# Value products of a head in two query tiles instead of three, and its output product in the same head

## The chip, the cores and the metric

The kernel runs on one core of a Trainium2 chip. The metric is the device time of one execution in microseconds, and lower is better. The core's engines work in parallel, each through its own queue in program order: TensorE (PE, with weight loads shown as PEld), VectorE (DVE), ScalarE (ACT), GpSimd (POOL) and SyncE (SP, which issues most DMAs).

## The reference

Three layers follow each other: a masked attention, a mixture of eight experts with one expert a token, and a gated feed-forward layer. The change touches the first, whose core is

```
q, k, v: (2, 8, 768, 64)                 # batches, heads, tokens, width of a head
mask   = bucket(q) == bucket(k)          # 6 hash bits of a token: (q @ proj > 0)
scores = where(mask, q @ k.T / 8, -1e9)
attn   = exp(scores - max); attn = attn / (sum + 1e-9)
out    = attn @ v                        # becomes x (1536, 512) of the experts
logits = x @ w_gate; gates of the output: x @ w_output_gate
```

The router's choice of an expert (the largest logit) needs all eight heads of a batch.

## The kernel before

**Tiling of the attention.** The 16 heads (two batches of eight) run one after the other, each in six query tiles of 128 tokens, `t` = 0 to 5. A step `g = 6 h + t` of the main loop issues the work below in the order in which it is written; every engine runs its share in that order.

1. `scores(g + 1)`: four matmuls into one of two PSUM buffers (`ps_s`) for the next tile; hash bits ride in the product, so that tokens of other buckets come out far away. `smax(g + 1)` on DVE: a minimum over 768 columns (L166) and a small scaling (L167), both needed by the exponential.
2. In tile 1, `hash_mm` of the next head. In tiles 1, 3 and 5, value products of the head before (`av_step`, L203): two of its six key tiles each (`AV_AT`), which add up in one PSUM buffer, the only one of the pool `ps_a`. Each writes 64 columns of the array, two halves side by side.
3. In tile 4, `o_out(h - 2)`: the output product (L255), which undoes the transposition and adds the router's logits, into the only buffer of the pool `ps_m`, and its two products with 1/sum on DVE (L264, L265).
4. `tposes(g, half)`: six transposes (L188) of the tile's exponentials into two PSUM buffers, and their eviction on ACT (L192) or DVE (L194), as the table `K["ev"]` says for each of the twelve halves of a head (1 is DVE).
5. `side(pos)`: the exponential of the next tile on ACT (`sexp`, L175) ahead of the transposes' evictions (position 0, tiles 1, 3 and 5) or behind them (position 2, tiles 0, 2 and 4); the splits of a later head's q and k into a rounded part on ACT (`split_a`, L105) and a rest on DVE and POOL (`split_b`, L117 to L121).
6. In tile 5, behind the transposes, `o_evac(h - 1)`: the value products leave PSUM (L234), and the sums of the exponentials are inverted (L238, L239).

Transposes of a tile wait for its exponential, the exponential for the scaling, that for the minimum, that for the scores. The last head, 15, differs: value products of head 14 lie in its tiles 0, 1 and 2, output products in tiles 0 and 3, and its own value products follow in tiles 4 and 5.

Between these lie the small operations of the router of the first batch (`todo`, one entry a tile from head 10, tile 2), and from head 14 on copies, splits and weight splits on POOL and ACT for the second stage (`extra`). Where POOL shall not begin before DVE's scaling is done, a copy of one column into `held` stands ahead of it.

Of the kernel before, what the change touches and what calls it, by code (L numbers as in the profile page):

```python
# [7 lines left out]
F32 = mybir.dt.float32  # L8
# [7 lines left out]
ALU = mybir.AluOpType  # L16
# [5 lines left out]
S, D, NB, NH = 768, 64, 2, 8  # L22
NT = 6
N, DM, E, FF, F2 = 1536, 512, 8, 1024, 1536
C = 224
GR = ((0, 6), (6, 4), (10, 2))
K = {'se': (2, 0, 2, 0, 2, 0), 'se0': (0, 1, 2, 1, 1, 2), 'ev': (0, 0, 0, 1, 0, 1, 0, 0, 0, 0, 1, 0), 'ev0': (0, 0, 0, 1, 0, 1, 0, 0, 0, 1, 0, 0), 'ev1': (0, 0, 0, 1, 0, 1, 0, 0, 0, 1, 0, 1), 'avl': (5,), 'oul': 0, 'hml': 0, 'hc': ((0, 0), (0, 2), (1, 1), (2, 1)), 'sa': ((0, 2), (2, 2)), 'sb': ((1, 0), (2, 2)), 'sa0': ((2, 2), (4, 1)), 'sb0': ((3, 2), (5, 0)), 'hm0': 0, 'hc0': ((1, 0), (1, 2), (3, 0), (4, 1))}
C_ID, C_TRI, C_THR, C_REV, C_TOK, C_IOTA, C_BASE, C_SLOT = 0, 128, 256, 258, 266, 278, 279, 287
CW = C_SLOT + C
FAR = 1024.0  # L30
AV_AT = {1: (0, 1), 3: (2, 3), 5: (4, 5)}


@with_exitstack
def attn_moe_kernel(ctx: ExitStack, tc: tile.TileContext, xin, cst, projd, wblk, wmoe, w2in, out):
# [127 lines left out]
    def smax(g):  # L163
        m = mm[:, g % 4]
        sb = sm.tile([128, 2], F32, tag="sb", name="sb")
        DVE.tensor_reduce(out=m[:, 1:2], in_=st[g][:, :, :384], axis=AX.XY, op=ALU.min)  # L166
        DVE.scalar_tensor_tensor(  # L167
            out=sb, in0=m[:, 1:2].to_broadcast([128, 2]), scalar=BIG / 2, in1=m, op0=ALU.is_le, op1=ALU.mult
        )
        scl[g], nbs[g] = sb[:, 0:1], sb[:, 1:2]  # L170
        last[0] = sb[:, 0:1]
# [24 lines left out]
    av = {}  # L196
# [21 lines left out]
    def halves(ap):  # L218

        return ap.bitcast(U16).rearrange("p t (n a) -> p t a n", a=2)  # L220

    def to_planes(t0, nt, hh, src):
        o = x_q.bitcast(U16).rearrange("p t (a n) -> p t a n", a=2)[:, t0:t0 + nt, :, hh * 64:(hh + 1) * 64]
        POOL.tensor_copy(o, src)

    def late_planes(hh, t0=0, nt=6):
        to_planes(t0, nt, hh, halves(x_b)[:, t0:t0 + nt, :, hh * 64:(hh + 1) * 64])
# [3 lines left out]
    def o_evac(h, q=None, copy=DVE.tensor_copy):  # L231
        n = q[1] * 128 if q else 384
        o = sm.tile([128, n], F32, tag="o" if q is None else f"o{n}", name="o", bufs=2 if q is None else 1)
        copy(o, av.pop((h, q) if q else h)[:, :n])  # L234
        oT[h, q] = o
        t0, nt = q or (0, NT)
        r = sm.tile([128, NT], F32, tag="r", name="r", bufs=2)
        DVE.tensor_reduce(out=r[:, :nt], in_=sums[:, h * 6 + t0:h * 6 + t0 + nt], axis=AX.X, op=ALU.add)  # L238
        DVE.reciprocal(r[:, :nt], r[:, :nt])  # L239
        rs[h, q] = r  # L240

    def o_out(h, q=None):
        b, hh = divmod(h, NH)
        o, r = oT.pop((h, q)), rs.pop((h, q))
        p = ps_m.tile([128, 512], F32, tag="m", name="m")
        t0, nt = q or (0, NT)
        t = slice(b * 6 + t0, b * 6 + t0 + nt)
        lp = sm.tile([128, nt, 16], F32, tag=f"lp{nt}", name="lp", bufs=2) if hh else lg[:, t]
        if b:
            xo = x_b[:, t0:t0 + nt, hh * 64:(hh + 1) * 64]  # L250
        else:
            xf = xo = sm.tile([128, 6, 64], F32, tag="xf", name="xf", bufs=2)
        if q is None:
            for j in range(3):
                PE.matmul(p[:, j * 160:(j + 1) * 160], o[:, j * 128:(j + 1) * 128], wb[:, hh], start=True, stop=True)  # L255
            ps = p[:, :480].rearrange("p (j c n) -> p j c n", j=3, c=2)
            rr = r.rearrange("p (c j) -> p j c", c=2).unsqueeze(3)
            lo, xo, sh = lp.rearrange("p (c j) n -> p j c n", c=2), xo.rearrange("p (c j) n -> p j c n", c=2), [128, 3, 2]
        else:
            for j in range(nt):  # L260
                PE.matmul(p[:, j * 80:(j + 1) * 80], o[:, j * 128:(j + 1) * 128], wl, start=True, stop=True)
            ps = p[:, :nt * 80].rearrange("p (j n) -> p j n", j=nt)
            rr, lo, sh = r[:, :nt].unsqueeze(2), lp, [128, nt]
        DVE.tensor_tensor(out=lo, in0=ps[..., 64:], in1=rr.to_broadcast(sh + [16]), op=ALU.mult)  # L264
        DVE.tensor_tensor(out=xo, in0=ps[..., :64], in1=rr.to_broadcast(sh + [64]), op=ALU.mult)  # L265
        if hh:
            (DVE if hh >= NH - 2 else POOL).tensor_tensor(out=lg[:, t], in0=lg[:, t], in1=lp, op=ALU.add)
        if not b:
            to_planes(0, 6, hh, halves(xf))
        elif NH + 3 <= h < L:  # L270
            late_planes(hh)

    def router(gi):
        t0, n = GR[gi]
# [362 lines left out]
    with tc.manual_schedule():  # L637
# [72 lines left out]
        L = NHD - 1  # L710
# [4 lines left out]
                f()  # L715
            return g

        parts = []

        def split_behind(d):  # L720
            def g():
# [18 lines left out]
        for g in range(NG):  # L740
            h, t = divmod(g, NT)
            if t == 1 and h + 3 < NHD:
                load(h + 3)
            if g + 1 < NG:
                scores(g + 1)
                smax(g + 1)
            if g < NT:
                set_up(g)
            if 2 * NT <= g < 2 * NT + (E * C + N) // 256:
                for i in (g - 2 * NT,):  # L750
                    nc.sync.dma_start(
                        out=xr[i * 256:(i + 1) * 256].rearrange("(p r) d -> p r d", p=128),
                        in_=zeros[0].bitcast(U32).unsqueeze(1).to_broadcast([128, 2, 512]),
                    )
            if g == 6 * NT:
                for n in range(4):
                    for part in range(2):
                        w_load(n, part)
            if g == 10 * NT + 1:
                r = router(0)  # L760
                todo = [r["s1"], r["s1b"], None, lambda: (r["s2"](), r["s2c"]()), r["s2b"], r["s4"], r["s4b"]]
                for f in r["sc"]:
                    todo += [f, None]
                todo += [r["s4c"], None, None, None, r["s3a"], None, r["s3b"], None, None, None, r["s5"]]
            early, late = [], []
            if h < L:
                if t == (1 if h else 0):
                    early.append(lambda: hash_mm(h + 1))
                if h:
                    for k in AV_AT.get(t, ()):  # L770
                        early.append(lambda k=k: av_step(h - 1, k))
                if h > 1 and t == 4:
                    (late if K["oul"] else early).append(lambda: o_out(h - 2))
            elif t < 3:
                av_step(h - 1, 2 * t)
                av_step(h - 1, 2 * t + 1)
                if t == 0:
                    o_out(h - 2)
                if t == 2:
                    o_evac(h - 1)  # L780
            elif t == 3:
                o_out(h - 1)
            else:
                k = 3 * (t - 4)
                av_group(h, qa, (k, k + 1, k + 2))
                if t == 5:
                    o_evac(h, qa)
            for f in early:
                f()
            if h and h < L and t == 5 and not K["avl"].count(5):  # L790
                o_evac(h - 1)
            if g > 10 * NT + 1 and todo:
                f = todo.pop(0)
                if f:
                    f()

            def side(pos):
                if g + 1 < NG and K["se" if 0 < h < L else "se0"][t] == pos:
                    sexp(g + 1)
                if h < L and (t, pos) == (1, 0):  # L800
                    hash_codes(h + 1)
                for i in range(2):
                    if h + 2 < NHD and K["sa" if h > 1 else "sa0"][i] == (t, pos):
                        split_a(h + 2, i)
                    if h + 2 < NHD and K["sb" if h > 1 else "sb0"][i] == (t, pos):
                        if t == 5:
                            POOL.tensor_copy(held, last[0])
                        split_b(h + 2, i)

            side(0)  # L810
            tposes(g, 0)
            side(1)
            tposes(g, 1)
            for f in late:
                f()
            if h and h < L and t == 5 and K["avl"].count(5):
                o_evac(h - 1)
            side(2)
            for f in extra.get((h - L + 1, t), ()):
                f()  # L820
        o_out(L, qa)
        av_group(L, qb, tuple(range(NT)))
        ra, rb = router(1), router(2)
        ra["s1"]()
# [11 lines left out]
        ra["s2c"]()  # L836
        for t in (6, 7, 8):
            x0_hot(DVE, t)
        o_out(L, qb)
        for t in (6, 7, 8):  # L840
            x0_add(t)
        rb["s1"]()
# [659 lines left out]
```

## Time and profile before

| | |
|---|---|
| median of 3 runs | 722.79 us (722.61 to 722.83) |
| profiled execution | 724.47 us |
| its span, first to last instruction | 722.7 us |
| mean granted clock of TensorE | 0.994 |
| PE, DVE, ACT, POOL busy | 705.2, 556.8, 448.1, 283.4 us |

All but the first line come from one profiled execution, which is 1.7 us longer than the median. Busy times are shares of the whole span, of which the attention stage is the first third; the ends of matmuls are modelled, so that the starts of instructions say more of PE than its busy time.

### The profile page before, as it was taken

Reading aid. Unit: us, or ns where it says so; the run is one execution under the profiler, and the core shown is the slowest. Engines: PE = TensorE matmul, PEld = TensorE weight load, DVE = VectorE, ACT = ScalarE, POOL = GpSimd, SP = SyncE. Lnnn points to the kernel's source line nnn. Section 1 sums busy time; section 2 is a strip of 40 time slices with the busy share of each in tenths; the row PEclk is TensorE's granted clock in tenths of the full one; section 3 lists DMA queues with packets and bytes.
Section 4 is the critical chain, followed back from the end, with each engine's and each line's share of the span. In section 5 each row is a group of like instructions: output and inputs, shape, how many; then the busy total and the mean of one; then the engine's idle time right before and its main releaser. Section 6 shows DMA issues by size and latency. Waiting matters only on the chain.

```text
span 722.7 us, 13158 instructions
## 1 busy us (share of the span) xinstructions
PE 705.2 (98%) x4505; PEld 604.2 (84%) x4506; DVE 556.8 (77%) x1105; ACT 448.1 (62%) x962; POOL 283.4 (39%) x316
## 2 busy tenths in 40 slices
PE   7899999999999999999999999999999999999995
PEld 6667667667766699999999999999999999999994
DVE  5777887789777778788888878886886877777644
ACT  5787877787877637677778766575444453444320
POOL 4243334322556348845443303333322332223224
PEclk9999999999999999999999999999999999999998
DMA  7348261123212038699899741132121222122013
GB/s 241 107 164 308 85 222 59 59 65 112 104 49 64 15 128 254 174 257 213 237 288 245 229 129 59 40 107 88 59 62 55 88 76 71 55 63 59 0 51 127
DMA packets 53432, 88.01 MB, mean 122 GB/s; under 512 B 19872, under 2 KB 23280, under 8 KB 53360
## 3 DMA queue, kind: packets, MB, share of 16 engines
q1 hardware_dynamic: 50688, 80.61, 37.7%
q0 software_dynamic: 2304, 6.31, 2.3%
q8 instruction: 37, 0.61, 0.3%
q14 instruction: 35, 0.29, 0.1%
q10 hardware_dynamic: 368, 0.20, 0.1%
HBM read 69.65 MB, written 13.12 MB: 115 GB/s over the span
## 4 chain that ended last, share of the span: by engine, by line
PE 84%; issue 4%; DVE 4%; POOL 2%; DMA 2%; ACT 2%; SPq 0%; POOLq 0%; ACTq 0%; DVEq 0%
PE tp L188 9%; PE av L203 8%; PE y L1033 6%; PE s L161 4%; PE s L160 4%; PE h L995 4%; PE h L994 4%; PE h L993 3%; PE aba L1270 3%; PE aba L1272 3%; PE abb L1270 3%; PE aba L1271 3%; PE abb L1272 3%; PE abb L1271 3%; PE y L1034 3%
## 5 line engine op out<-in xcount | busy, mean ns | idle before, releaser
L166 DVE TENSOR_REDUCE mm<-s 128x1 f32<-128x768 f32 x96 | 91.1, 949 | 26.7 <-PE s L161 25.8
L175 ACT ACTIVATE p<-s,sb 128x768 f32<-128x768 f32 x96 | 95.0, 989 | 21.2 <-DVE sb L167 20.4
L188 PEld LDWEIGHTS tp<-cs,p 128*128 128x128 f32 x576 | 64.9, 141 | 37.9 <-ACT p L175 24.4
L188 PE MATMUL tp<-cs,p 128*128 128x128 f32 x576 | 82.7, 280 | 6.4 <-DMA cs<-cst 2.9
L516 DVE TENSOR_TENSOR wl<-wr,wh 128x512 fp32r<-128x512 f32 x125 | 83.2, 705 | 4.9 <-ACT wh L515 1.1
L192 ACT ACTIVATE pt<-tp 128x384 f32<-128x384 f32 x143 | 65.1, 487 | 34.7 <-PE tp L188 34.7
L964 POOL TENSOR_TENSOR pc<-t,pc 128x256 fp32r<-128x256 f32 x38 | 33.1, 873 | 134.8 <-ACT pc L963 119.2
L1033 PE MATMUL y<-hl,wh 128*128 128x448 f32 x224 | 75.0, 378 | 0.6 <-DVE hl L1007 0.5
L515 ACT ACTIVATE wh<-wr 128x512 fp32r<-128x512 f32 x128 | 73.7, 624 | 1.3 <-DMA wr<-wmoe 1.2
L160 PE MATMUL s<-tk,tq 76*128 76x384 f32 x192 | 73.7, 384 | 0.3 <-DVE tq L137 0.3
L994 PE MATMUL h<-xl,wh 128*128 128x224 f32 x256 | 70.3, 275 | 0.5 <-DVE xl L450 0.3
L995 PE MATMUL h<-xh,wl 128*128 128x224 f32 x256 | 70.6, 276 | 0.0
L993 PE MATMUL h<-xh,wh 128*128 128x224 f32 x256 | 70.3, 275 | 0.2 <-ACT xh L449 0.2
L203 PE MATMUL av<-pt,v 128*64 128x384 f32 x360 | 68.0, 499 | 0.2 <-DVE r L238 0.2
L161 PE MATMUL s<-bk,bq 128*128 128x384 f32 x192 | 65.6, 342 | 0.0
L1034 PE MATMUL y<-hl,wl 128*128 128x224 f32 x224 | 59.5, 266 | 0.0
L964 POOL TENSOR_TENSOR pc<-s,pc 128x256 fp32r<-128x256 f32 x44 | 38.0, 875 | 33.0 <-ACT pc L963 32.0
L118 POOL CAST bq<-tq 64x768 fp32r<-64x768 f32 x15 | 21.2, 1414 | 74.8 <-ACT tq L105 47.4
L1160 ACT ACTIVATE gh<-p 128x384 fp32r<-128x384 f32 x21 | 11.0, 526 | 63.2 <-DVE p L1289 63.2
L993 PEld LDWEIGHTS h<-xh,wh 128*128 128x128 f32 x256 | 48.9, 191 | 1.5 <-ACT xh L449 0.4
L994 PEld LDWEIGHTS h<-xl,wh 128*128 128x128 f32 x256 | 49.1, 192 | 1.0 <-DVE xl L450 0.5
L203 PEld LDWEIGHTS av<-pt,v 128*64 128x64 f32 x360 | 21.9, 136 | 32.8 <-issue 24.5
(264 smaller groups left out, 2002.6 us busy)
## 6 DMA issues: line engine op xcount, KB each, us to landing
wr<-wmoe SPq DMA_DIRECT2D x128, 256.0 KB
r<-w2in SPq DMA_DIRECT2D x36, 512.0 KB
x<-xin SPq DMA_DIRECT2D x30, 384.0 KB
xr<-zero SPq DMA_DIRECT2D x13, 512.0 KB
v<-xin SPq DMA_DIRECT2D x16, 192.0 KB
wb<-wblk SPq DMA_DIRECT2D x1, 640.0 KB
x<-xin SPq DMA_DIRECT2D x3, 192.0 KB
tq<-code SPq DMA_DIRECT2D x30, 18.0 KB
```

The costliest lines, as they stand in the source:

```text
L160: PE.matmul(p[:, c, :384], T[h, 0][:76, qs], T[h, 1][:76, sl], start=True, stop=False)
L161: PE.matmul(p[:, c, :384], B[h, 0][:, qs], B[h, 1][:, sl], start=False, stop=True)
L166: DVE.tensor_reduce(out=m[:, 1:2], in_=st[g][:, :, :384], axis=AX.XY, op=ALU.min)
L175: ACT.activation(p.rearrange("p (c n) -> p c n", c=2), st.pop(g)[:, :, :384], ACTF.Exp, scale=scl.pop(g), bias=nbs.pop(g), accum_out=sums[ ...
L188: PE.transpose(ps[:, j * 128:(j + 1) * 128], pt_[g][:, k * 128:(k + 1) * 128], ident)
L203: PE.matmul(av[h][c * 64:(c + 1) * 64, :384], v, PT[h][:, k, c * 384:(c + 1) * 384], start=(k == 0), stop=(k == NT - 1), skip_group_check= ...
L516: eng.tensor_tensor(out=l, in0=r, in1=h.bitcast(F32), op=ALU.subtract)
L993: PE.matmul(ps, wh, xh, start=first, stop=False)
L994: PE.matmul(ps, wh, xl, start=False, stop=False)
L995: PE.matmul(ps, wl, xh, start=False, stop=last)
L1033: PE.matmul(p, wh[:, w], hl, start=(f == 0), stop=False, skip_group_check=True)
L1034: PE.matmul(p[:, 0], wl[:, w], hl[:, 0], start=False, stop=(f == 7), skip_group_check=True)
```

## The change

- Value products of the head before go into tiles 1 and 3 alone, three key tiles each.
- `o_evac` follows directly behind the second group, in tile 3; within it the sums come ahead of the copy.
- The output product goes to tile 5 of the same head (`o_out(h - 1)` instead of `o_out(h - 2)`), ahead of the transposes, and for heads 0 to 13 into the buffer of `ps_a` that held the value products. Its products on DVE are returned as a function `take` and issued in tile 0 of the next head, behind the minimum and scaling there.
- In tile 5 both evictions are on DVE (before one on DVE, one on ACT).
- The split of k's rest goes from position 2 of tile 2 to position 0 of tile 3, with the `held` copy ahead of it; the latter is now also placed in tile 3 of heads 0 and 1.
- The router's operations begin two tiles earlier.

```
-K = {... 'ev': (0, 0, 0, 1, 0, 1, 0, 0, 0, 0, 1, 0), ... 'sb': ((1, 0), (2, 2)), ...}
+K = {... 'ev': (0, 0, 0, 1, 0, 1, 0, 0, 0, 0, 1, 1), ... 'sb': ((1, 0), (3, 0)), ...}
-AV_AT = {1: (0, 1), 3: (2, 3), 5: (4, 5)}
+AV_AT = {1: (0, 1, 2), 3: (3, 4, 5)}
...
     def o_evac(h, q=None, copy=DVE.tensor_copy):
-        copy(o, av.pop((h, q) if q else h)[:, :n])
...
         rs[h, q] = r
+        copy(o, av.pop((h, q) if q else h)[:, :n])
...
     def o_out(h, q=None):
-        p = ps_m.tile([128, 512], F32, tag="m", name="m")
+        if h < L - 1:
+            p = ps_a.tile([128, 512], F32, tag="a", name="m")
+        else:
+            p = ps_m.tile([128, 512], F32, tag="m", name="m")
...
-        DVE.tensor_tensor(out=lo, in0=ps[..., 64:], in1=rr.to_broadcast(sh + [16]), op=ALU.mult)
-        DVE.tensor_tensor(out=xo, in0=ps[..., :64], in1=rr.to_broadcast(sh + [64]), op=ALU.mult)
...
+        def take():
+            DVE.tensor_tensor(out=lo, in0=ps[..., 64:], in1=rr.to_broadcast(sh + [16]), op=ALU.mult)
+            DVE.tensor_tensor(out=xo, in0=ps[..., :64], in1=rr.to_broadcast(sh + [64]), op=ALU.mult)
...
+        return take
...
                 scores(g + 1)
                 smax(g + 1)
+            if t == 0 and takes:
+                takes.pop()()
...
-            if g == 10 * NT + 1:
+            if g == 9 * NT + 5:
...
-                if h > 1 and t == 4:
-                    (late if K["oul"] else early).append(lambda: o_out(h - 2))
+                if h and t == 3:
+                    early.append(lambda: o_evac(h - 1))
+                if h and t == 5:
+                    early.append(lambda: takes.append(o_out(h - 1)))
             elif t < 3:
                 av_step(h - 1, 2 * t)
                 av_step(h - 1, 2 * t + 1)
-                if t == 0:
-                    o_out(h - 2)
...
-            if h and h < L and t == 5 and K["avl"].count(5):
-                o_evac(h - 1)
```

## Rows read from the trace of the kernel before

**Rows 1.** Windows of head 6, tiles 1, 2, 4, 5: stretch, length, then each engine.

```profile
101.41:105.14 3.73, 3.73 (x28) 1.91 (x28) 3.34 (x7) 3.46 (x8) 1.14 (x1) 1.00 0.33 101
105.14:106.50 1.36, 1.36 (x11) 1.33 (x11) 1.21 (x2) 0.58 (x2) 0.42 (x1) 1.00 1.01 384
...
109.45:111.64 2.19, 2.19 (x18) 2.19 (x18) 1.60 (x3) 1.53 (x6) 2.02 (x2) 1.00 0.00 0
111.64:114.60 2.96, 2.96 (x20) 1.75 (x20) 2.15 (x6) 2.42 (x6) 1.21 (x2) 1.00 0.02 6
```

**Rows 2.** Timeline of PE in tiles 4 and 5: start, duration, instructions merged.

```profile
109.63 0.34 PE L161 MATMUL s<-bk,bq 128*128 128x384 f32 x1
109.81 0.98 PE L255 MATMUL m<-wb,o 128*128 128x160 f32 x6
110.62 0.82 PE L188 MATMUL tp<-cs,p 128*128 128x128 f32 x6
...
111.81 0.34 PE L161 MATMUL s<-bk,bq 128*128 128x384 f32 x1
```

**Rows 3.** Timeline of all engines: a softmax from its last score matmul, then value products.

```profile
105.31 0.34 PE L161 MATMUL s<-bk,bq 128*128 128x384 f32 x1
...
105.69 0.96 DVE L166 TENSOR_REDUCE mm<-s 128x1 f32<-128x768 f32 x1 [0.15 <-PE s L161]
...
106.68 0.16 DVE L167 SCALAR_TENSOR_TENSOR sb<-mm 128x2 f32<-128x2 f32 x1
106.76 0.55 DVE L194 COPY pt<-tp 128x384 f32<-128x384 f32 x1
106.94 0.99 ACT L175 ACTIVATE p<-s,sb 128x768 f32<-128x768 f32 x1 [0.43 <-DVE sb L167]
...
107.32 0.14 PEld L203 LDWEIGHTS av<-pt,v 128*64 128x64 f32 x2 [0.18 <-issue]
107.64 0.14 PEld L203 LDWEIGHTS av<-pt,v 128*64 128x64 f32 x2 [0.18 <-issue]
```

**Rows 4.** Timeline in head 14, where transposes waited for the exponential.

```profile
224.69 0.99 ACT L175 ACTIVATE p<-s,sb 128x768 f32<-128x768 f32 x1 [1.06 <-DVE sb L167]
...
225.83 0.44 PE L188 MATMUL tp<-cs,p 128*128 128x128 f32 x2 [0.25 <-ACT p L175]
```

**Rows 5.** Timeline of head 6: POOL's cast, the scaling, the output's second product.

```profile
110.71 0.82 POOL L121 CAST bk<-tk 64x768 fp32r<-64x768 f32 x1
111.00 0.55 DVE L167 SCALAR_TENSOR_TENSOR sb<-mm 128x2 f32<-128x2 f32 x1
...
111.64 0.54 DVE L265 TENSOR_TENSOR xf<-m,r 128x384 f32<-128x384 f32 x1
```

**Rows 6.** Windows of heads 1, 10 and 11, 12, and 14 with tile 0 of 15.

```profile
28.33:43.18 14.85, 14.08 (x93) 9.31 (x93) 10.49 (x19) 11.60 (x25) 4.03 (x5) 1.00 0.32 109
...
159.62:189.39 29.77, 29.66 (x207) 20.69 (x206) 25.93 (x59) 23.07 (x48) 11.19 (x10) 1.00 0.26 90
...
189.39:203.96 14.57, 14.57 (x100) 10.26 (x99) 11.43 (x23) 11.39 (x25) 7.57 (x7) 1.00 0.36 128
218.52:236.08 17.56, 17.14 (x114) 11.61 (x113) 12.86 (x28) 13.63 (x31) 12.37 (x19) 1.00 0.21 65
```

**Rows 7.** Timeline of heads 14 and 15: cast, two subtractions on POOL, router.

```profile
230.31 0.63 ACT L515 ACTIVATE wh<-wr 128x512 fp32r<-128x512 f32 x1
...
231.03 1.28 POOL L516 TENSOR_TENSOR wl<-wr,wh 128x512 fp32r<-128x512 f32 x1 [0.26 <-ACT wh L515]
...
232.40 1.81 POOL L398 TENSOR_TENSOR xh<-x_b,xh 128x768 fp32r<-128x768 f32 x1
...
238.26 0.19 DVE L372 TENSOR_REDUCE rt_s<-rt_ed 128x6 f32<-128x48 f32 x1
```

**Rows 8.** Windows of head 0: stretch, length, busy times; third from last: granted clock.

```profile
11.21:14.63 3.42, 0.60 (x6) 0.63 (x7) 1.68 (x3) 2.08 (x5) 2.21 (x2) 1.00 1.01 389
14.63:18.04 3.41, 3.41 (x16) 3.31 (x15) 1.71 (x4) 1.92 (x4) 1.77 (x4) 0.50 0.83 260
```

More of the change, by code (lines that the diff above doesn't have):

```diff
@@ L26 @@
 GR = ((0, 6), (6, 4), (10, 2))
-K = {'se': (2, 0, 2, 0, 2, 0), 'se0': (0, 1, 2, 1, 1, 2), 'ev': (0, 0, 0, 1, 0, 1, 0, 0, 0, 0, 1, 0), 'ev0': (0, 0, 0, 1, 0, 1, 0, 0, 0, 1, 0, 0), 'ev1': (0, 0, 0, 1, 0, 1, 0, 0, 0, 1, 0, 1), 'avl': (5,), 'oul': 0, 'hml': 0, 'hc': ((0, 0), (0, 2), (1, 1), (2, 1)), 'sa': ((0, 2), (2, 2)), 'sb': ((1, 0), (2, 2)), 'sa0': ((2, 2), (4, 1)), 'sb0': ((3, 2), (5, 0)), 'hm0': 0, 'hc0': ((1, 0), (1, 2), (3, 0), (4, 1))}
+K = {'se': (2, 0, 2, 0, 2, 0), 'se0': (0, 1, 2, 1, 1, 2), 'ev': (0, 0, 0, 1, 0, 1, 0, 0, 0, 0, 1, 1), 'ev0': (0, 0, 0, 1, 0, 1, 0, 0, 0, 1, 0, 0), 'ev1': (0, 0, 0, 1, 0, 1, 0, 0, 0, 1, 0, 1), 'hml': 0, 'hc': ((0, 0), (0, 2), (1, 1), (2, 1)), 'sa': ((0, 2), (2, 2)), 'sb': ((1, 0), (3, 0)), 'sa0': ((2, 2), (4, 1)), 'sb0': ((3, 2), (5, 0)), 'hm0': 0, 'hc0': ((1, 0), (1, 2), (3, 0), (4, 1))}
 C_ID, C_TRI, C_THR, C_REV, C_TOK, C_IOTA, C_BASE, C_SLOT = 0, 128, 256, 258, 266, 278, 279, 287
@@ L263, in o_out @@
             rr, lo, sh = r[:, :nt].unsqueeze(2), lp, [128, nt]
-        DVE.tensor_tensor(out=lo, in0=ps[..., 64:], in1=rr.to_broadcast(sh + [16]), op=ALU.mult)
-        DVE.tensor_tensor(out=xo, in0=ps[..., :64], in1=rr.to_broadcast(sh + [64]), op=ALU.mult)
[L266 to L271, printed above, removed]
+        def take():
+            DVE.tensor_tensor(out=lo, in0=ps[..., 64:], in1=rr.to_broadcast(sh + [16]), op=ALU.mult)
+            DVE.tensor_tensor(out=xo, in0=ps[..., :64], in1=rr.to_broadcast(sh + [64]), op=ALU.mult)
+            if hh:
+                (DVE if hh >= NH - 2 else POOL).tensor_tensor(out=lg[:, t], in0=lg[:, t], in1=lp, op=ALU.add)
+            if not b:
+                to_planes(0, 6, hh, halves(xf))
+            elif NH + 3 <= h < L:
+                late_planes(hh)
+        return take
     def router(gi):
@@ L716, in behind @@
             return g
-        parts = []
+        parts, takes = [], []
         def split_behind(d):
@@ L764, in attn_moe_kernel @@
                 todo += [r["s4c"], None, None, None, r["s3a"], None, r["s3b"], None, None, None, r["s5"]]
-            early, late = [], []
+            early = []
             if h < L:
@@ L781, in attn_moe_kernel @@
             elif t == 3:
-                o_out(h - 1)
+                o_out(h - 1)()
             else:
@@ L789, in attn_moe_kernel @@
                 f()
-            if h and h < L and t == 5 and not K["avl"].count(5):
-                o_evac(h - 1)
-            if g > 10 * NT + 1 and todo:
+            if g > 9 * NT + 5 and todo:
                 f = todo.pop(0)
@@ L805, in side @@
                     if h + 2 < NHD and K["sb" if h > 1 else "sb0"][i] == (t, pos):
-                        if t == 5:
+                        if t in (3, 5):
                             POOL.tensor_copy(held, last[0])
@@ L813, in attn_moe_kernel @@
             tposes(g, 1)
-            for f in late:
-                f()
-            if h and h < L and t == 5 and K["avl"].count(5):
-                o_evac(h - 1)
             side(2)
@@ L820, in attn_moe_kernel @@
                 f()
-        o_out(L, qa)
+        o_out(L, qa)()
         av_group(L, qb, tuple(range(NT)))
@@ L838, in attn_moe_kernel @@
             x0_hot(DVE, t)
-        o_out(L, qb)
+        o_out(L, qb)()
         for t in (6, 7, 8):
```

## The prediction

> **What bounds the kernel now.** I read the page first: TensorE (PE) is shown busy for 705.2 of 722.7 us, but ends of matmuls are modelled there, so this alone doesn't say that nothing is lost. The change touches only the attention stage, which runs from about 9 to 250 us. I therefore cut one settled head into its query tiles, with the windows laid from one score matmul to the next tile's [rows 1]. The reader should see that each tile's length is a plain sum: a tile with scores and transposes alone takes 1.36 us; one with an output product as well 2.19; one with value products of two key tiles 2.96; the one with the hash product and value products 3.73. The two tiles not shown take 1.36 and 2.95, and the head 14.57 us. Then I followed PE in order of time through the same head [rows 2]: group follows group with no hole. So in a settled head PE sets the pace, and the other engines have slack: DVE 11.4 and ACT 11.4 of 14.57 us [rows 6]. Such a head gets faster only if PE gets less to do, and slower as soon as a result comes late for PE.
>
> **What the change takes away.** Value products write 64-column blocks of the array, the groups around them full width. Two key tiles are four pairs of matmuls, a pair every 0.32 us (weight loads at 107.32 and 107.64 [rows 3]), 1.28 in all, yet the tile grows by 2.96 - 1.36 = 1.60 us [rows 1]. So 0.32 us is paid for going in and out of such a group. Before there are three groups a head, after two with three key tiles each. The bounds are 0.28 and 0.34; I take 0.32, in 14 heads (1 to 14): -4.5 us.
>
> **What it moves together.** The work of PE is now uneven: tiles 1 and 3 (the second and fourth) carry all value products, tile 5 only the output product (2.19 - 1.36 = 0.83 us), tiles 4 and 0 nothing. Between the last score matmul of tile 5's scores and its first transpose lie: transposes of tile 4, the next scores, the output product. From rows: score to the next full-width group 0.18 (109.63 to 109.81), transposes and scores 111.81 - 110.62 = 1.19, last score through the output product to the transposes 110.62 - 109.63 = 0.99; together 2.36 us [rows 2]. Before, a value group lay in it as well.
>
> What must happen in that time is the softmax: the minimum on DVE starts 0.38 us after the last score matmul, takes 0.96, the small scaling ends at 106.84, the exponential starts at 106.94 and takes 0.99 [rows 3]: 1.63 to its start, 2.62 to its end. Where PE waited for nothing else, transposes start 0.15 us after the exponential's end [rows 4]. That makes 2.77 us with no queue at all. So PE waits 2.77 - 2.36 = 0.41 us ahead of the transposes of tile 5, in every one of the 14 heads: +5.7 us. The bounds are 0.35 (a few hundredths less at each hand-over) and 0.8: the scaling ends late when GpSimd (POOL) is in the middle of an instruction, as at 111.00, where it took 0.55 instead of 0.16 and ended as POOL's cast did [rows 5]. There the cast ended (111.53) 1.90 us after the scores of tile 5; with two more pairs of value products ahead of these scores (0.64) that becomes 1.26, and the scaling starts at 0.38 + 0.96 + 0.03 = 1.37, so they miss each other by 0.1 us. The next tile's softmax has the same 2.77 us and comes out just in time, behind the same wait.
>
> The rest of the edits costs nothing in a settled head. The seventh DVE eviction of a head (0.55 [rows 3]) and its partner fall into that wait, and end as the next minimum can start. The products on DVE, put off to tile 0, follow that minimum and scaling and end 1.53 [rows 3] + 0.63 [rows 5] = 2.16 us after their scores; the value products, which need their PSUM buffer, come at 1.36 + 0.18 + the hash product's 3.73 - 2.96 = 2.31 at the earliest. That cover is 0.15 us; without it each tenth goes to PE. The evacuation in tile 3 is on DVE behind nothing but the end of the value products, and the next minimum is queued behind it 0.9 us later. POOL's split in tile 3 starts when ACT has delivered, as before. So a settled head goes from 14.57 to 14.57 - 0.32 + 0.41 = 14.66 us.
>
> **Where heads are not settled.** Heads 2 to 9, 12 and 13: 10 x 0.09 = +0.9 us. Heads 10 and 11 hold the router's small operations, and take 29.77 us together [rows 6], 0.63 more than two settled ones. Moved forward two tiles, its matmuls on PE stay (0.2, an estimate: a third of the 0.63), and its DVE work falls where there is room: 2 x 14.66 + 0.2 = 29.52, -0.2. Head 1 had no output product and waits (14.85 [rows 6]); now it has one, and ACT's split of 768 columns lies between two evictions in tile 4, ahead of the exponential. I estimate it at 0.7 us, since a cast of 512 takes 0.63 [rows 7]. The wait there is then about 1.0 instead of 0.41: 15.25, +0.4.
>
> Head 14 with tile 0 of head 15 is dearer. There the value products are still in tile 0, directly behind the scores, and now they need the buffer that the put-off products are to free. Counted from the scores of tile 5: the second minimum of head 15 starts after four small router operations (about 0.85 us in a chain, the first with 0.19 is shown [rows 7]) and two evictions, at 4.8, and ends at 5.7. Its scaling meets POOL: the exponential ends at 2.6, ACT's cast (0.63) follows, POOL's subtraction (1.28) and its next one (1.81) [rows 7] run until 6.6. The products take 0.63 more after the scaling (111.55 to 112.18 [rows 5]): the buffer is free at 7.3, while PE could start at 4.2. PE waits 3.1 us; without meeting POOL it is 2.4. The page SBUF — State Buffer of the Trainium skill, section Who interferes with whom, says that a DVE operation with two SBUF inputs and a POOL operation that reads SBUF exclude each other for a whole instruction; [rows 5] agree for a cast, and for the longer subtraction the rule gives the 3.1. A scaling that didn't wait would give the 2.4, and a sum smaller by 0.7 us. The stretch took 17.56 [rows 6], with 0.6 of waits of its own in it that go; after: 14.66 + 1.60 for the group in tile 0 + 3.13 = 19.39, +1.8.
>
> **The sum.** +0.9 - 0.2 + 0.4 + 1.8 = +2.9 us. After the attention stage a chain follows that starts from its last tiles, so nothing catches this up. The profiled execution took 724.47 us with a span of 722.7; its successor should take 727.4. The runs had a median of 722.79, and the same difference gives 725.7.
>
> **Rivals.**
> The waits ahead of tile 5 are hidden (ends on the other side). Then 14 x 0.41 = 5.7 us fall away: 720.0. It decides from 0.21 us a head down, where the total is nil. For it: before, no settled head waits. Against it: the 2.77 us are counted on rows without a queue, and PE can't fill 2.36 us with more than it has.
>
> The wait in head 15 is small, because the put-off products reach DVE earlier than I have them. With 3.1 us gone the total is -0.2, 722.6; with half gone 724.1, both about unchanged. For it: it rests on the order in four queues that I put together by hand. Against it: even an idle POOL leaves 2.4 us.
>
> The clock falls in that wait. TensorE was granted 1.00 up to 14.63 us and 0.50 (1.2 of 2.4 GHz) from there to 18.04, after a stretch in which it was busy for 0.60 of 3.42 us [rows 8]. Three idle microseconds in head 15 resemble that. PE's work of 3.41 us at half the clock costs 1.7 more: 727.4. The page TensorE: Matmul & The Clock Gate of the Trainium skill, Part 1, has the clock throttled by default and released by activity, which the two rows agree with; by that rule this change is dangerous in that place only. Against it: scores stand close ahead of the wait and value products behind it.
>
> POOL's cast does meet the scaling in tile 5, by a tenth of slip. It costs up to 0.39 more in some 12 heads: +4.7, 730.4. Only the margin of 0.1 us speaks against it.
>
> **How the numbers follow.** Within 0.2% (1.4 us) is about what a measurement can't tell from no change. The forecast (724.3 to 727) has 0.47, the fallen clock 0.15, the meeting with POOL 0.06: slower 0.68. The small wait in head 15 has 0.15, and I add 0.05 for errors that cancel: same 0.20. The hidden waits have 0.12. The range leaves out those and the meeting with POOL: from 722.4, below the small wait, to 728.3, above the fallen clock with the forecast's own error. The likeliest case's own range is 724.3 to 727.
>
> **What would show it.** Tiles of a settled head should last 1.36, 4.38, 1.36, 3.59, 1.36 and 2.59 us. Transposes of tile 5 should start 0.15 us after the exponential's end, with PE idle some 0.4 us ahead. In head 15 the first value products should start right behind the put-off products on DVE, some 3 us late. The prediction is wrong if tile 5 takes 2.2 us, if the value products in head 15 aren't held, or if the heads 2 to 9 lose much more than a tenth each.

## The result, and the profile after

The changed kernel takes 733.36 us (median of 4 runs, 730.8 to 734.59) against 722.81 us for the kernel before: the ratio is 1.0142, with a 95% interval of 1.0114 to 1.0169. It is slower, as forecast, but by 10.5 us instead of 2.9, and outside the range. The profiled execution took 733.75 us with a span of 731.9.

I cut the same head as in [rows 1] into windows, one from the last score matmul of a tile to that of the next (tiles 1, 2, 3, 4, 5 and 0).

```profile
102.18:106.56 4.38, 4.38 (x32) 2.20 (x31) 3.95 (x8) 3.59 (x7) 2.03 (x3) 1.00 0.44 158
106.56:107.93 1.37, 1.37 (x12) 1.33 (x11) 1.18 (x3) 0.49 (x1) 0.00 (x0) 1.00 0.68 247
107.93:111.53 3.60, 3.60 (x24) 2.04 (x24) 2.47 (x7) 3.35 (x7) 1.58 (x2) 1.00 0.05 9
111.53:112.89 1.36, 1.36 (x12) 1.33 (x11) 0.96 (x1) 0.86 (x3) 1.26 (x2) 1.00 0.04 12
112.89:115.53 2.64, 2.39 (x18) 2.15 (x17) 1.94 (x5) 2.22 (x5) 0.00 (x0) 1.00 0.00 0
115.53:116.99 1.46, 1.46 (x12) 1.27 (x11) 1.35 (x3) 0.82 (x4) 0.00 (x0) 1.00 0.00 0
```

Four tiles are what was forecast (4.38, 1.36, 3.59, 1.36), and tile 5 is the only one in which PE isn't busy throughout. The head takes 14.81 us instead of 14.55. Tile 5 in the timeline, PE with what it waits for (start, duration, instructions merged):

```profile
112.89 0.34 PE L161 MATMUL s<-bk,bq 128*128 128x384 f32 x1
...
112.89 0.16 DVE L167 SCALAR_TENSOR_TENSOR sb<-mm 128x2 f32<-128x2 f32 x1
113.06 0.98 PE L258 MATMUL m<-wb,o 128*128 128x160 f32 x6
113.15 0.99 ACT L175 ACTIVATE p<-s,sb 128x768 f32<-128x768 f32 x1
...
114.29 0.88 PE L188 MATMUL tp<-cs,p 128*128 128x128 f32 x6 [0.25 <-ACT p L175]
114.32 0.16 DVE L167 SCALAR_TENSOR_TENSOR sb<-mm 128x2 f32<-128x2 f32 x1
114.60 0.99 ACT L175 ACTIVATE p<-s,sb 128x768 f32<-128x768 f32 x1 [0.37 <-DVE sb L167]
```

From the output product to the transposes it is 1.23 us, where it was 0.81 [rows 2]: the wait is 0.42, and the transposes start 0.15 us after the exponential's end at 114.14. They take 0.88 us instead of 0.82. The exponential of tile 0 starts 0.12 us after its scaling and ends at 115.59; the transposes of tile 0 start 0.14 us behind it, at 115.73, and tile 0 is 0.09 longer as well.

The dearest place is tile 0 of head 15:

```profile
235.97 0.33 PE L161 MATMUL s<-bk,bq 128*128 128x384 f32 x1
...
236.65 1.80 POOL L405 TENSOR_TENSOR xh<-x_b,xh 128x768 fp32r<-128x768 f32 x1
...
237.49 0.98 DVE L167 SCALAR_TENSOR_TENSOR sb<-mm 128x2 f32<-128x2 f32 x1
...
238.56 0.54 DVE L270 TENSOR_TENSOR x_b<-m,r 128x384 f32<-128x384 f32 x1
...
239.24 2.19 PE L203 MATMUL av<-pt,v 128*64 128x384 f32 x6 [2.94 <-DVE x_b L270]
...
239.91 0.27 PEld L203 LDWEIGHTS av<-pt,v 128*64 128x64 f32 x2 [0.37 <-issue]
...
240.55 0.27 PEld L203 LDWEIGHTS av<-pt,v 128*64 128x64 f32 x2 [0.37 <-issue]
```

The value products wait for the put-off products, and those for a scaling that lasts 0.98 us and ends when POOL's subtraction does (238.45). The pairs then follow each other 0.64 us apart, twice the 0.32 of [rows 3]. Windows over that place show what else changed there (the third value from the end is the granted clock):

```profile
234.49:237.90 3.41, 1.57 (x10) 1.26 (x10) 3.04 (x10) 2.42 (x6) 2.62 (x3) 1.00 0.06 10
237.90:241.31 3.41, 2.07 (x8) 0.85 (x8) 1.20 (x3) 1.08 (x2) 3.09 (x6) 0.50 0.18 67
241.31:244.73 3.42, 3.42 (x14) 2.31 (x10) 0.00 (x0) 0.98 (x2) 0.16 (x1) 0.50 0.00 0
```

PE's clock was granted at 0.50, 1.2 of 2.4 GHz, for 6.8 us, after a stretch in which it was busy for 1.57 of 3.41 us. Head 1 and heads 10 and 11 together, to be held against the first two of [rows 6], 14.85 and 29.77 us:

```profile
27.25:42.73 15.48, 14.71 (x99) 10.30 (x99) 11.06 (x20) 11.11 (x23) 4.34 (x6) 1.00 0.31 104
161.60:192.51 30.91, 29.85 (x206) 20.77 (x206) 26.42 (x63) 22.74 (x45) 10.82 (x13) 1.00 0.26 87
```

With the start of the last score matmul of each head's tile 2 as the border, the attention stage grows by 0.63 us in head 1, 2.43 in heads 2 to 9, 1.14 in heads 10 and 11, 0.69 in heads 12 and 13, and 4.42 in head 14 with tile 0 of head 15: 9.3 us. Behind that lie 1.2 us more, half of them behind the last matmul. The two spans differ by only 9.2, because the profiled execution of before took 1.25 us more up to that border in head 1; its clock was low there [rows 8], and that of after was not.

### The profile page after: what moved, and what is told of

Read it like the earlier page. It is cut to its first block, busy times and chain, and to the rows that moved or that the text cites. A ratio compares the mean times of both kernels' runs of the same rounds, so it can differ in the third digit from the quotient of the medians.

```text
span 731.9 us, 13181 instructions
## 1 busy us (share of the span) xinstructions
PE 707.0 (97%) x4505; PEld 606.0 (83%) x4506; DVE 561.1 (77%) x1119; ACT 446.4 (61%) x948; POOL 278.1 (38%) x330
## 4 chain that ended last, share of the span: by engine, by line
PE 78%; POOL 5%; DVE 5%; issue 5%; ACT 4%; DMA 1%; SPq 0%; POOLq 0%; ACTq 0%; DVEq 0%
PE av L203 8%; PE tp L188 8%; PE y L1036 5%; PE s L160 4%; PE s L161 3%; PE aba L1273 3%; PE h L998 3%; PE aba L1275 3%; PE abb L1273 3%; PE aba L1274 3%; PE abb L1275 3%; PE abb L1274 3%; PE h L996 3%; PE h L997 3%; PE q L1203 3%
## 5 line engine op out<-in xcount | busy, mean ns | idle before, releaser
L175 ACT ACTIVATE p<-s,sb 128x768 f32<-128x768 f32 x96 | 95.0, 990 | 19.9 <-DVE sb L167 15.6
L192 ACT ACTIVATE pt<-tp 128x384 f32<-128x384 f32 x129 | 58.5, 488 | 45.9 <-PE tp L188 45.6
L203 PE MATMUL av<-pt,v 128*64 128x384 f32 x360 | 66.2, 503 | 3.1 <-DVE x_b L270 2.9
L203 PEld LDWEIGHTS av<-pt,v 128*64 128x64 f32 x360 | 23.5, 138 | 37.8 <-issue 30.1
L998 PEld LDWEIGHTS h<-xh,wl 128*128 128x128 f32 x256 | 49.2, 192 | 0.0
```

The source lines that it names most:

```text
L175: ACT.activation(p.rearrange("p (c n) -> p c n", c=2), st.pop(g)[:, :, :384], ACTF.Exp, scale=scl.pop(g), bias=nbs.pop(g), accum_out=sums[ ...
L203: PE.matmul(av[h][c * 64:(c + 1) * 64, :384], v, PT[h][:, k, c * 384:(c + 1) * 384], start=(k == 0), stop=(k == NT - 1), skip_group_check= ...
L998: PE.matmul(ps, wl, xh, start=False, stop=last)
```

## The experiments

The kernel before ran beside each of them. Its median was 723.96 us beside the first three runs told here and the one with work put into the wait; 723.46 beside the runs on the second eviction of tile 4, the value products alone, the router's old place and the earlier scores; 723.16 beside the two with spread steps and the eviction given back; and 723.17 beside the two with steps in DVE's gaps. Ratios are to that kernel.

**The wait in head 15 taken away.** The output product of head 13 uses the pool `ps_m`, as before the change, so that the value products of head 14 wait for nobody.

```
-        if h < L - 1:
+        if h < L - 2:
             p = ps_a.tile([128, 512], F32, tag="a", name="m")
```

> The changed kernel with the output product of head 13 in its own PSUM buffer, so that the value products in tile 0 of head 15 need not wait for the put-off products. If that wait of 3 us and the half clock behind it are a part of the loss, 4 to 6 us come back: 727.5 to 729.5 us, no stretch of half clock near 238 us, tile 0 of head 15 at about 3 us instead of 8.3. If the loss there has another cause (a late exponential, POOL's work), PE waits for that instead and at most 1 us comes back.

727.85 us, ratio 1.0062 (1.0045 to 1.0078). Tile 0 of head 15, 8.33 us long in the changed kernel, falls to its plain work, and the clock stays:

```profile
235.95:238.91 2.96, 2.96 (x20) 1.75 (x19) 2.83 (x6) 1.27 (x3) 2.69 (x4) 1.00 0.24 89
```

So this one place costs 5.4 us, half of the whole loss. To part wait and clock, the next run keeps the wait and fills it.

**The wait kept, the clock held.** 48 matmuls into an unread buffer stand ahead of the value products in tile 0 of head 15.

```
+                if t == 0:
+                    busy = ps_m.tile([128, 512], F32, tag="m", name="busy")
+                    for _ in range(48):
+                        PE.matmul(busy[:, :128], ones, ones, start=True, stop=True)
                 av_step(h - 1, 2 * t)
```

> The changed kernel with 48 small matmuls, whose result nobody reads, ahead of the value products in tile 0 of head 15: some 2.7 us of work in the place of the wait. If the wait is for the put-off products, the value products start no later. If the fall of the clock costs something of its own, it no longer falls, and 2 to 3 us come back: 730 to 731.5 us. If the clock costs nothing beyond the wait, the time stays at 733.

731.6 us, ratio 1.011 (1.0092 to 1.0128), a tenth above the 730 to 731.5 us expected. The window of the tile in this kernel:

```profile
235.11:241.07 5.96, 5.73 (x67) 4.52 (x67) 2.99 (x6) 2.67 (x6) 5.18 (x8) 1.00 0.13 47
```

The value products still wait 0.23 us for the put-off products behind the 48 matmuls, so the added work is no longer than the wait. 5.96 - 2.96 = 3.0 us is the wait, as forecast (3.13), and 8.33 - 5.96 = 2.4 us went with the clock that fell. Here it stays at 1.00.

The 2.4 us are one execution's. The run further down with work put into the wait has the same code in head 15 and the same wait of 3.0 us, and its tile 0 took 7.55 us, 1.6 more than with the clock held:

```profile
236.70:244.25 7.55, 4.62 (x19) 2.84 (x19) 2.99 (x6) 2.99 (x6) 5.17 (x8) 0.77 0.13 35
```

Its clock was at 0.50 for 3.4 us instead of 6.8. In the two runs with a shorter minimum the tile took 7.47 and 7.40 us. So the clock cost 1.4 to 2.4 us in four executions with the same wait.

**The softmax of tiles 5 and 0 made shorter.** The minimum is taken over half of the columns there, in heads 1 to 15.

```
+        c = 1 if g % NT in (0, 5) and g > NT else 2
-        DVE.tensor_reduce(out=m[:, 1:2], in_=st[g][:, :, :384], axis=AX.XY, op=ALU.min)
+        DVE.tensor_reduce(out=m[:, 1:2], in_=st[g][:, 2 - c:, :384], axis=AX.XY, op=ALU.min)
```

> The changed kernel with the minimum of the scores taken over 384 of the 768 columns in tiles 5 and 0 of heads 1 to 15: this leaves out half of the maximum, and shortens the softmax there by 0.4 us. If the waits ahead of the transposes of tiles 5 and 0 (0.41 us, and 0.14 by two smaller ones) make a settled head 14.81 instead of 14.24, most of it goes: tile 5 at 2.2 to 2.3 us, tile 0 at 1.36 to 1.4, a head at 14.25 to 14.4, the run at 726 to 728. If PE or another engine sets the pace, a head stays at 14.8 and the run at 733.

729.47 us, ratio 1.0087 (1.0064 to 1.011): a settled head takes 14.56 us, so only half of what was expected came. The minimum is 0.40 shorter, but the scaling of tile 5 takes 0.37 us instead of 0.16 and ends with POOL's cast (111.86 and 111.85), and the exponential starts 0.12 us behind it, after two evictions on ACT. The next run takes one of these evictions away.

**The second eviction of tile 4 on DVE, on top of that.**

```
-'ev': (0, 0, 0, 1, 0, 1, 0, 0, 0, 0, 1, 1)
+'ev': (0, 0, 0, 1, 0, 1, 0, 0, 0, 1, 1, 1)
```

> The changed kernel with the shorter minimum of the run before (384 columns in tiles 5 and 0, half of the maximum left out), and besides with the second eviction of tile 4 on DVE instead of ACT. If two chains of almost equal length reach the exponential of tile 5, one over the minimum and one over the two evictions that stand ahead of it on ACT, then both are now shorter: tile 5 falls from 2.49 to 2.2 us and a settled head to 14.24 to 14.3. If the rest of the wait has another cause, tile 5 stays at 2.5.

727.75 us in the one run, and 14.52 us a head instead of 14.24 to 14.3: a second miss. Its timeline shows what still holds the exponential:

```profile
109.90 0.82 POOL L121 CAST bk<-tk 64x768 fp32r<-64x768 f32 x1
...
110.38 0.36 DVE L168 SCALAR_TENSOR_TENSOR sb<-mm 128x2 f32<-128x2 f32 x1
...
110.83 0.99 ACT L176 ACTIVATE p<-s,sb 128x768 f32<-128x768 f32 x1 [0.23 <-DVE sb L168]
110.95 0.98 PE L259 MATMUL m<-wb,o 128*128 128x160 f32 x6
...
111.97 0.44 PE L189 MATMUL tp<-cs,p 128*128 128x128 f32 x2
```

With an earlier minimum the scaling meets POOL's cast, the rival that I had at 0.06, and ends with it (110.74 and 110.72). The wait is still 1.02 - 0.81 = 0.21 us; in the changed kernel the cast ends 0.04 us before the scaling starts.

**Work put into the wait.** Seven matmuls into an unread buffer in tile 5 of heads 2 to 13.

```
+            if t == 5 and 1 < h < L - 1:
+                busy = ps_m.tile([128, 512], F32, tag="m", name="busy")
+                for _ in range(7):
+                    PE.matmul(busy[:, :128], ones, ones, start=True, stop=True)
```

> The changed kernel with 7 small matmuls (about 0.39 us of PE's time, result unread) behind the output product in tile 5 of heads 2 to 13. If PE waits there anyway for the exponential, a head stays at 14.8 and the run within 1 us of the changed kernel. If PE's own work sets the pace, each of the 12 heads grows by 0.4 and the run by 4.7 us.

732.84 us, ratio 1.0119 (1.0096 to 1.0141), with settled heads of 14.81 us to the hundredth. PE had nothing to do there.

**The value products moved alone.** The kernel before with two groups of three key tiles and nothing else of the change.

```
-AV_AT = {1: (0, 1), 3: (2, 3), 5: (4, 5)}
+AV_AT = {1: (0, 1, 2), 3: (3, 4, 5)}
```

> The kernel before with the value products in tiles 1 and 3 alone, and nothing else of the change: the output product stays in tile 4. One group less saves 0.32 us a head, but the exponential of tile 5 then waits behind evictions of transposes that the output product holds up, and nothing covers it: PE waits about 1.0 us ahead of tile 5 and 0.15 to 0.25 ahead of tile 0, a settled head takes 15.4 to 15.6 us, and the run 10 to 13 us more than the kernel before. If the gaps were a matter of the other edits, the head would take 14.25 and the run 4 us less.

738.37 us, ratio 1.0212 (1.0192 to 1.0231). Tiles 5 and 0 of a settled head:

```profile
116.52:119.00 2.48, 1.59 (x12) 1.26 (x11) 1.78 (x4) 1.94 (x4) 0.87 (x2) 1.00 0.00 0
119.00:120.68 1.68, 1.64 (x12) 1.25 (x11) 1.54 (x5) 1.42 (x5) 0.00 (x0) 1.00 0.00 0
```

The run takes 14.9 us more than the kernel before, where 10 to 13 were expected, and a head 15.69 us instead of 15.4 to 15.6. Without the output product tile 5 has 1.36 us of work and takes 2.48. So the other edits together give 0.88 us a head back. I put that down to the output product, which now covers tile 5, but no run moves it alone.

**The router begun where it was before,** on the kernel with the wait in head 15 taken away (`g == 10 * NT + 1`). The last scatter of the first batch then moves rows over which head 11's put-off products have been written, so those rows differ.

> The kernel with the output product of head 13 in its own buffer, and with the router's operations begun at head 10, tile 2, as before the change. If their place two tiles earlier is what makes heads 10 and 11 long (15.7 each), these fall to 15.0 to 15.2 and the run by about 1 us against the run with the buffer alone. If the operations cost the same in either place, nothing changes.

728.47 us, ratio 1.0068 (1.0049 to 1.0086), which can't be told from the 1.0062 with the earlier start. Heads 10 to 12 take 47.16 us; with the earlier start they take 45.73 to 46.23 in the changed kernel and three runs that have its code there. Moving the router two tiles forward was not what made these heads slow.

**Scores of tiles 5 and 0 issued one group of transposes earlier,** with the router as in the run before (the same rows differ), POOL's cast behind, and the evictions dealt out anew.

```
+            if 0 < h < L and t in (3, 4):
+                scores(g + 2)
+                smax(g + 2)
```

> The changed kernel with the buffer of its own and the router as before the change, and with the scores of tiles 5 and 0 one group of transposes earlier, so that 0.6 us more of PE's work lies between scores and transposes there (their exponential ahead of the evictions, the second eviction of tile 4 on DVE instead of that of tile 5, POOL's cast behind the scaling of tile 5). If the waits are only the softmax coming late, they go and the saving of a group of value products is left: a settled head at 14.25 to 14.4 us, the run 2 to 4 us below the kernel before. If the waits come from the load of DVE, ACT or POOL, a head stays above 14.6.

723.61 us, ratio 1.0 (0.9987 to 1.0012): no gain over the kernel before, where 2 to 4 us were expected. A settled head takes 14.51 us, not the 14.25 that its groups add up to. What is late now is an eviction:

```profile
110.17 0.99 ACT L177 ACTIVATE p<-s,sb 128x768 f32<-128x768 f32 x1
...
111.15 0.48 ACT L194 ACTIVATE pt<-tp 128x384 f32<-128x384 f32 x1
...
111.68 0.90 PE L190 MATMUL tp<-cs,p 128*128 128x128 f32 x6
```

The transposes of tile 5 need the PSUM buffer that ACT empties behind the exponential which now comes earlier. That places 0.13 of the 0.26 us left: from the output product (110.74) to the transposes it is 0.94 instead of 0.81. About half of what a head lost is left, and a part of it has moved to another resource.

**Why heads 10 and 11?** In the changed kernel, the router's first operations, which DVE reaches in tile 1 of head 10, and what follows (timeline):

```profile
162.38 0.19 DVE L300 TENSOR_REDUCE rt_mx<-lg 128x6 f32<-128x48 f32 x1
...
162.97 0.95 DVE L166 TENSOR_REDUCE mm<-s 128x1 f32<-128x768 f32 x1
163.80 0.82 POOL L118 CAST bq<-tq 64x768 fp32r<-64x768 f32 x1 [6.53 <-ACT tq L105]
164.06 0.58 DVE L167 SCALAR_TENSOR_TENSOR sb<-mm 128x2 f32<-128x2 f32 x1
...
166.48 0.54 DVE L194 COPY pt<-tp 128x384 f32<-128x384 f32 x1
...
167.08 0.55 PE L188 MATMUL tp<-cs,p 128*128 128x128 f32 x3 [0.27 <-DVE pt L194]
```

DVE is almost full in tile 1 (3.95 of 4.38 us in the windows above). Three router operations delay the minimum, the scaling meets POOL's cast, three more router operations follow it, and an eviction comes late for PE: tile 2 takes 2.00 instead of 1.37 us. Head 11 loses in its tile 0, which takes 1.89 instead of 1.45 us:

```profile
185.20 0.97 POOL L466 DMA_INDIRECT xr<-x_q,pos_i  x1 [0.28 <-POOL bq L118]
...
188.19 1.81 POOL L120 TENSOR_TENSOR bk<-x,tk 64x768 fp32r<-64x768 f32 x1 [1.78 <-ACT pt L192]
...
189.41 0.59 DVE L167 SCALAR_TENSOR_TENSOR sb<-mm 128x2 f32<-128x2 f32 x1
```

Behind a scatter (L466) POOL begins the subtraction of k's rest 3.0 us later in the head than in head 6, where it starts at 110.13. The scaling of tile 0 then lasts until the subtraction ends (190.00). What POOL waited for before 188.19 isn't settled: this row names an eviction on ACT, the same row of the run with the clock held names the scatter's transfer. In three runs with the same code there, this tile takes 1.98 to 2.36 us. The last 0.22 us are the router's matmuls in tile 3 of head 10.

First I thought that tiles 4, 5 and 0 were the bad ones, and put one step or scatter into each of tiles 1, 2 and 3 of heads 9 to 12.

```
-            if g > 9 * NT + 5 and todo:
+            if g > 9 * NT and todo and t in (1, 2, 3):
```

> The first repair (output product of head 13 in its own buffer), and the first batch's router begun five tiles earlier, one small step or one scatter a tile, in tiles 1, 2 and 3 of heads 9 to 12 alone, whose softmax has value products as cover. Theory (heads 10 and 11 grew because the router's work on DVE and POOL falls into tiles 4, 5 and 0, where nothing covers the softmax any more): heads 10, 11 and 12 come back to the settled 14.8 us, at most 0.2 more where the router's matmuls stand; from 31.34 to about 29.8 for heads 10 and 11, 726.3 us in all. Rival (it is the router's own matmuls and its place on PE): heads 9 to 12 keep together what heads 10 and 11 had too much, about 1.7 us, and the time stays at 727.8.

730.8 us, ratio 1.0097 (1.008 to 1.0114): wrong. Heads 9 to 14 grew by 3.7 us against the run with the wait in head 15 taken away. The same on the arrangement with the earlier scores:

> The kernel with the scores of tiles 5 and 0 one group of transposes ahead, and the router as in the run beside it, so that each scatter again takes the rows that it should. By the theory heads 10, 11 and 12 (15.34, 15.05 and 14.92 us with the router in its old place) come to its settled 14.51, 1.8 us less: 721.8 us, 0.2% below the kernel before. By the rival the time stays at 723.5.

725.55 us, ratio 1.0026 (1.0015 to 1.0037), above the rival's 723.5 too, and heads 9 to 13 with 75.6 us. Head 10 of this kernel shows how a step in tile 3 does harm:

```profile
169.38 0.83 POOL L122 CAST bk<-tk 64x768 fp32r<-64x768 f32 x1
...
169.50 0.72 DVE L372 TENSOR_TENSOR pos_i<-pos,rt_p 128x6 int32<-128x6 f32 x1
...
170.14 0.94 DVE L168 TENSOR_REDUCE mm<-s 128x1 f32<-128x768 f32 x1
...
171.88 0.55 PE L190 MATMUL tp<-cs,p 128*128 128x128 f32 x3 [0.60 <-DVE pt L196]
```

A small operation lasts until POOL's cast ends, the minimum and the eviction behind it slip, and PE waits 0.60 us. So I took it that the place of each step in DVE's and POOL's queues counts, and not its tile's cover on PE. Two runs test that: short steps only where DVE was seen idle, none in tile 1 of heads 9 to 13, and the scatters at the end of tile 5, where POOL is idle. The first has the earlier scores, the second the arrangement of the changed kernel, with the output product of head 13 in its own buffer and one eviction given back to ACT.

```
+                todo = {
+                    (9, 2): ["s1"], (9, 3): ["s1m", "s1b"], (9, 5): ["s1c"], (10, 2): ["s2", "s2c"],
+                    (10, 3): ["s2b", "s4"], (10, 5): ["s4m", "s4b"], (11, 2): ["s4n"], (11, 5): r["sc"][:3],
+                    (12, 5): r["sc"][3:], (13, 3): ["s4c"], (14, 1): ["s3a"], (14, 3): ["s3b"], (15, 1): ["s5"],
+                }
```

> Scores of tiles 5 and 0 one group ahead, own buffer for the output product of head 13, and the first batch's router cut into steps of two or three small DVE operations, each where DVE stood idle for 0.3 to 0.5 us in the trace of that arrangement: in tile 2 ahead of the evictions, in tile 3 ahead of the sums, and at the end of tile 5; none in tile 1, where DVE is nearly full, and the six scatters on POOL at the end of tile 5 of heads 11 and 12, where POOL is idle for 3 us. Theory (heads 10 and 11 grow where a router step meets a full DVE, and where a scatter pushes POOL's split into a scaling): heads 9, 11, 12 and 13 take 14.5 to 14.6 us, head 10 0.4 more for its matmuls on PE; heads 9 to 13 together 73.0 instead of 75.6 us in the run with evenly spread steps, 721.5 us in all. Rival (the steps cost what they cost wherever they stand): 75 us for these heads, 724 to 725.5.

721.53 us, ratio 0.9974 (0.9963 to 0.9985): faster than both kernels, if only by a quarter of a per cent against the kernel before. Windows of heads 9 to 13:

```profile
143.55:158.06 14.51, 14.51 (x100) 10.39 (x99) 12.61 (x30) 11.45 (x23) 4.41 (x5) 1.00 0.22 75
158.06:172.88 14.82, 14.82 (x108) 10.56 (x108) 12.62 (x28) 11.38 (x23) 3.59 (x4) 1.00 0.22 72
172.88:187.40 14.52, 14.52 (x100) 10.39 (x99) 12.20 (x26) 11.44 (x23) 6.37 (x8) 1.00 0.27 93
187.40:201.91 14.51, 14.51 (x99) 10.39 (x99) 12.10 (x23) 11.32 (x23) 7.06 (x9) 1.00 0.37 132
201.91:216.42 14.51, 14.51 (x99) 10.38 (x99) 11.80 (x24) 11.31 (x23) 5.79 (x7) 1.00 0.11 38
```

Together 72.87 us, against 75.63 with the steps spread evenly. All of the router's DVE work is in there at no price that these heads show; head 10 has 0.31 more, and eight matmuls more, than head 9.

> The change with the output product of head 13 in its own buffer and the second eviction of tile 5 on ACT, and the router's steps in the same places as in the run beside it. By the theory heads 9 to 13, which took 14.86, 15.61, 15.33, 15.21 and 14.86 us with the router as the change has it, come to 14.86 each and 0.4 more in head 10: 74.7 instead of 75.9, 1.2 us less than the 726.6 of that kernel. By the rival 75.9 and 726.6.

Heads 9 to 13 took 74.79 us, as the theory had it (74.7), against 75.88 with the router as the change has it. The whole took 727.19 us, ratio 1.0046 (1.0029 to 1.0064), no less than the 726.59 of the one run, told of next, with which it is compared, where 1.2 us less were expected. The profiled execution of the 727.19 kernel, with 729.1 us, lost 1.9 us before head 2 begins, where the edit does nothing and its clock was 0.77 and 0.73 in two stretches between 18.0 and 24.8 us; so the heads tell more here than the totals. Both runs moved steps and scatters together, so they don't part what either cost.

**The eviction given back to ACT,** on the kernel with the wait in head 15 taken away.

```
-'ev': (0, 0, 0, 1, 0, 1, 0, 0, 0, 0, 1, 1)
+'ev': (0, 0, 0, 1, 0, 1, 0, 0, 0, 0, 1, 0)
```

> The first repair, and the second eviction of tile 5 back on ACT, as before the change. My prediction costs this edit at nothing, since the eviction falls into the wait. If that holds, a settled head keeps 14.81 us. The other reading: on ACT it stands behind the exponential of tile 0, which ends 1.4 us after the first transposes of tile 5, and the transposes of tile 0 wait for the buffer that it empties; then a settled head takes about 0.3 us more, and the edit was worth that much to the change.

726.59 us in one run. A settled head takes 14.87 instead of 14.81 us, and heads 5, 9 and 13 as much as the others, where the changed kernel has 15.01. So the eviction on DVE gains 0.06 us in most heads and loses 0.14 in those three: about nothing, as forecast.

## Why the prediction was wrong

The direction and the main mechanism were right: two groups instead of three leave tile 5 without cover, and PE waits for its softmax. The tiles of a settled head came out at 4.38, 1.37, 3.60 and 1.36 us as forecast; the wait ahead of tile 5's transposes at 0.42 us against 0.41. What failed is the sum around it. It held one wait a head where there are two, it put the clock in head 15 and the router's place on DVE at nothing, and it closed at the end of the attention stage. The 7.6 us between 2.9 and 10.5 lie at five places, the largest share (2.6) in head 14 with tile 0 of head 15:

- **Heads 2 to 9, 12 and 13: +3.1 instead of +0.9 us.** "14.57 - 0.32 + 0.41 = 14.66 us" held one wait alone, and called the next softmax "just in time, behind the same wait". Its 14.57 was head 12's length; the six tiles of head 6 add up to 14.55. The saving was 0.30. Behind the wait the transposes take 0.05 longer and tile 0 0.09: 14.81. The rest, 0.2 in each of heads 5, 9 and 13, is told below. The hidden-waits rival was refuted by the filled wait: 14.81 us with and without seven more matmuls.
- **Heads 10 and 11: +1.1 instead of -0.2.** "Its DVE work falls where there is room" was the step that failed here. It was not looked up in DVE's own order: [rows 1] show 3.34 us of DVE work in 3.73 us of tile 1. Nor did the sum hold the scatters, which push POOL's subtraction into a scaling. Of the 1.29 us above two settled heads, 0.63 lie in tile 2 of head 10, 0.44 in tile 0 of head 11, and 0.22 on PE as estimated (0.2). With steps and scatters in the gaps of DVE and POOL, heads 9 to 13 lost 1.09 us less in the arrangement of the changed kernel.
- **Head 14 with tile 0 of head 15: +4.4 instead of +1.8.** The wait, put together from four queues, was right (3.0 against 3.13): counted from the scores of tile 5 (231.87), the subtraction ended after 6.58 us against 6.6, and the buffer was free after 7.23 (my 6.6 + 0.63 is 7.2, not 7.3). The step that failed is that the sum put the clock behind this wait at nothing. It was a rival with a chance of 0.15 and a price of 1.7 us, and it happened, for 2.4 us in the profiled execution and 1.4 to 1.6 in three other runs; the other 0.35 lie in head 14's own tiles. The low clock in head 0 [rows 8] was the hint that I weighed too little. By the rule of the Trainium skill that I had named (TensorE: Matmul & The Clock Gate, Part 1) this place was the dangerous one, and the trace agrees: busy for 1.57 of 3.41 us, then 0.50. The scaling that lasts 0.98 us until POOL's subtraction ends agrees with the page SBUF — State Buffer of the Trainium skill, section Who interferes with whom, and so with the longer of my two waits.
- **Head 1: +0.6 instead of +0.4.** Tile 5 took 3.16 us. The estimate of 0.7 for ACT's split was too small (0.84), and the sum had nothing for tile 4, which took 1.61 us instead of 1.36.
- **Behind head 15's tile 0: +1.2 instead of 0.** Some 0.6 of it lies behind the last matmul. The profiled executions of the thirteen other kernels have between 0.2 us less and 2.0 us more than before in this stretch, so one execution of each kernel doesn't show that the change costs anything there; it stays open.

The rival that POOL's cast meets the scaling didn't come true in the changed kernel, where they miss each other by 0.04 us, but did in both runs with a shorter minimum. In the settled heads no wait of PE for the edits around the value products shows; of these edits only the eviction was tested by itself, at about nothing.

## What to carry to other kernels

Before work of PE is put together into fewer places, count for each tile what is left between the scores and the first use of their softmax: the tile that becomes bare sets the time, and what is saved at the groups must pay for it. A wait of some microseconds on PE has to be priced with the clock that may fall behind it (here 1.4 to 2.4 us on top of 3.0), and small operations on another engine by the gaps in that engine's own queue, an instruction at a time. A put-off consumer of a single PSUM buffer should have a buffer of its own: one line here was worth half of the loss (5.5 of 10.5 us).

## What the runs showed that I had not expected

- The clock stayed at 0.50 through a whole stretch (241.31 to 244.73) in which PE was busy throughout, so that a wait of 3.0 us cost 5.4. With the same wait the other executions lost 4.4 to 4.6; the runs don't say what decides between them.
- In heads 5, 9 and 13 of the changed kernel the exponential of tile 5 starts 0.33 us after all that the trace shows it to need, and in the others 0.05 us. The same shows in the runs with the first repair and with the half minimum, and not in the runs where evictions on ACT were dealt out otherwise. The cause stays open. Head 5, the scaling and the exponential:

```profile
97.88 0.16 DVE L167 SCALAR_TENSOR_TENSOR sb<-mm 128x2 f32<-128x2 f32 x1
...
98.42 0.99 ACT L175 ACTIVATE p<-s,sb 128x768 f32<-128x768 f32 x1 [0.33 <-ACT pt L192]
```

- Transposes that follow the wait took 0.88 us where six take 0.82 behind scores or an output product. In the kernel before they take 0.88 behind value products too (113.53 in head 6), with no wait shown, so it is not shown that the wait is the reason.
